# Ten high-half casts of weight pairs move from GpSimd to ScalarE, and the first pair of W_in is loaded and converted first

## The chip, the core and the metric

The kernel runs on one core of a Trainium2 chip. The core has TensorE (PE: matmuls; PEld: its weight loads), VectorE (DVE), ScalarE (ACT) and GpSimd (POOL), which run their own instruction streams in order and wait for each other by semaphores. SyncE (SP) issues all DMA transfers here. The metric is the time of one execution on the device in microseconds (us); "before" is the median of three runs.

## The reference

Attention with a decay and a causal mask, then two MLPs, over 4 x 576 tokens of 8 heads of 64:

```python
scores = np.where(causal, -1e9, scale * q @ k^T + cum[:, None] - cum[None, :])
x  = softmax(scores) @ v                 # (2304, 512)
h  = x @ w_in                            # w_in  (512, 2048)
g  = h * np.tanh(np.where(h > 20, h, np.log1p(np.exp(h))))
x2 = g @ w_out                           # w_out (2048, 512)
h2 = x2 @ w2_in                          # (512, 1024)
solu = h2 * softmax(h2)
out = layernorm(solu) * g_ln @ w2_out    # (1024, 512)
```

The weights come as float64, q, k, v and f as float32.

## The kernel before

Every matmul operand is kept as a pair of float16 halves, high and low (value = high + low), and each product is made of three matmuls: high x high, high x low, low x high.

**Weights.** W_in and W_out of the first MLP are cut into eight *pairs* each (two tiles of 128 x 512). A pair goes through three steps of class `Weight`. `load` brings the float64 values in with one DMA of 1,024 KB (L123); only two such buffers exist (`WB = 2`), shared by both weights, so a load waits until the conversion before the last has freed its buffer. `conv` makes float32 of the two 32-bit words of each float64 with three DVE instructions (L136, L138, L140) and then sums squares on PE (`gram`, L159). `split` scales the pair and makes its two halves by the function `split`, in one of three modes, chosen per pair by a digit of the strings `W1P` (W_in) and `W2P` (W_out):

- mode 0: ACT makes the scaled high half (L197), DVE the low half (L198);
- mode 1: ACT scales in place (L200), POOL casts the high half (L202), POOL subtracts to get the low half (L205);
- mode 2: as mode 1, but ACT casts the high half (L204).

The same function splits q, k and v. The scales of a group of four pairs (`bound`) come from `gram`.

**Order.** The code first issues loads of k, q, two pairs of W_in and v of the first batch, then the statistics of k (`stats`, `scales`), the splits of k and q, and starts attention. All other weight steps stand in a list `wsteps` that alternates two pairs of W_in and two of W_out; `wgo(n)` takes the next n steps, between attention steps. The first token block of the MLP (`up`: matmuls L754; `mish_a` to `mish_c`: L766 to L781; `down`: L798) is interleaved with these weight steps, since it needs them group by group. Later blocks of the MLP are interleaved with attention of the other batches, and the second MLP (lines about 1000) with the last ones. The program order is then rearranged by a scheduler in the build, which orders each engine's stream by its own model of time; the streams run on the chip exactly in that order.

Names: `win`, `wout` are the weights (the tile `wout` also lends its unused space to early k, q, v rows), `wi_r`, `wo_r` the float64 buffers, `kn`, `qn` the split k and q before their DMA transposes into `kt`, `qa`; `p`, `ph`, `pT` attention probabilities, their halves and their transposes; `h`, `ta`, `th`, `gt` the MLP's hidden values.

Of the kernel before, what the change touches and what calls it, by code (L numbers as in the profile page):

```python
# [40 lines left out]
WPF = 2  # L41
# [8 lines left out]
HI0 = "a"  # L50
HI1 = "pd"
SP1 = "0000001"
W1P = "00111111"
W2P = "10"
QKV = "002"
W0C = 1
S2Q = 3
S2R = 9
WB = 2
# [13 lines left out]
def rows_of(b, c):  # L73
    off = OFF[b]
    lo = max(128 * c, off)
    hi = min(128 * c + 128, off + S)
    return lo - 128 * c, hi - 128 * c, lo - off


def part_of(w, n):  # L80

    fr, c = divmod(2 * n, w.shape[0] // P)
    return w[c * P:(c + 2) * P, fr * 512:(fr + 1) * 512].rearrange("(s p) e -> p s e", p=P)


def later(tc, a, b):

    tc.add_manual_dep(
        getattr(a, "ins", a), getattr(b, "ins", b).name,
        mybir.DependencyInfo(mybir.DependencyClass.NoSync, mybir.DependencyReason.DATA),  # L90
        reason="issue order")
# [116 lines left out]
def emit(tc, q, k, v, f, w_in, w_out, w2_in, w2_out, g_ln, out):  # L208
# [81 lines left out]
    def load_raw(b, c, which, pool=None):  # L290
        r0, r1_, t0 = rows_of(b, c)
        n = r1_ - r0
        for nm in which:
            src = {"q": q, "k": k, "v": v}[nm]
            if pool is None:
                t = rawp.tile([P, DM], F32, tag="raw", name=f"raw{nm}_{b}_{c}")
            else:
                t = pool.pop()
            raw[nm, b, c] = t
            i = nc.sync.dma_start(  # L300
                t[r0:r1_].rearrange("p (h d) -> p h d", h=H),
                src[b, :, t0:t0 + n, :].rearrange("h s d -> s h d"),
            )
        return i

    def stats(b, c, which):

        if ("st", b) not in sc:
            sc["st", b] = att.tile([P, 2, NCH], F32, tag="st", name=f"st_{b}", bufs=2)
            nc.vector.memset(sc["st", b], 0.0)  # L310
        r0, r1_, _ = rows_of(b, c)
        for nm in which:
            jk = attd.tile([P, DM], F32, tag="x32", name=f"jk{nm}_{b}_{c}", bufs=1)
            nc.scalar.activation(
                jk[r0:r1_], raw[nm, b, c][r0:r1_], AF.Square,
                accum_out=sc["st", b][r0:r1_, "kv".index(nm), c:c + 1])
# [211 lines left out]
    def fin(b, i):  # L528
# [41 lines left out]
    W1 = Weight(  # L570
        tc, wst, "wi", win, NC1 * DFF // 512, lambda n: part_of(w_in, n), across, group=4,
        after=lambda: pend.get("pt"), gram=grams)
# [13 lines left out]
    def w1_split(n):  # L586
        g, r = divmod(n, W1.group)
        if r == 0:
            W1.bound(g)
            nc.vector.tensor_copy(wps[g], W1.p(g))  # L590
        W1.split(n, on_pool=int(W1P[n % len(W1P)]))

    def w2_split(n):
        g, r = divmod(n, W2.group)
        if r == 0:
            W2.bound(g)
            nc.vector.tensor_tensor(rho[:, g:g + 1], wps[g], W2.p(g), op=ALU.mult)
        W2.split(n, on_pool=int(W2P[n % len(W2P)]))

# [72 lines left out]
    wsteps, wdone = [], set()  # L672
    order = [(w, 2 * g + n) for g in range(4) for w in (W1, W2) for n in range(2)]
    for x in range(len(order) + WPF):
        if WPF <= x < len(order):
            wsteps.append((order[x][0].load, order[x][1]))
        if x >= WPF:
            w, n = order[x - WPF]
# [5 lines left out]
    def wgo(n):  # L684
        for _ in range(n):
            if wsteps:
                f, a = wsteps.pop(0)
                f(a)
                wdone.add((f, a))
# [7 lines left out]
    def pool0(c):  # L697
        return spare if c < 3 else None

    for c in range(NCH):  # L700
        load_raw(0, c, "k", pool0(c))
    for c in range(2):
        load_raw(0, c, "q", pool0(c))
    for n in range(WPF):
        W1.load(n)
    load_raw(0, 0, "v", pool0(0))
    for c in range(NCH):
        stats(0, c, "k")
    scales(0, "k")
# [6 lines left out]
    later(tc, load_raw(0, 2, "q", pool0(2)), first)  # L716
    wgo(W0C)
    for c in range(NCH):
# [156 lines left out]
    for hn in range(2 * (NF + 5)):  # L875
        n, half = divmod(hn, 2)
# [212 lines left out]
```

## Time and profile before

| | |
|---|---|
| median of three runs | 861.46 us (859.14 to 862.57) |
| profiled execution | 862.0 us, of which the span from first to last instruction is 860.2 us |
| busy, PE | 748.2 us (87% of the span) |
| busy, DVE | 606.7 us (71%) |
| busy, ACT | 549.1 us (64%) |
| busy, POOL | 442.2 us (51%) |
| mean granted clock of TensorE | 0.97 |

The shares are means over stages with different limits. The busy time of DVE and of POOL includes the time in which an instruction has started and is held up. About 1.8 us of the profiled time lie outside the span.

### The profile page before, as it was taken

What the parts mean: (1) busy time and instruction counts of PE and PEld (TensorE: products, weight loads), DVE (VectorE), ACT (ScalarE), POOL (GpSimd) and SP (SyncE); (2) the same over time, 40 slices, a digit from 0 to 9 for tenths busy, and PEclk for the clock granted to TensorE, in tenths of its full rate; (3) what the DMA queues carried; (4) which work ended last, traced back from release to release, by engine and by line L of the source; (5) the groups of instructions that cost most, each with busy time, mean ns of one, the idle gap of its engine ahead of it and who ended that gap; (6) DMA issues with size and microseconds to landing.
All of it is one profiled execution on the core that took longest, in us unless ns stands there. A gap on an engine that the chain in (4) does not pass through costs nothing.

```text
span 860.2 us, 16457 instructions
## 1 busy us (share of the span) xinstructions
PE 748.2 (87%) x6174; PEld 477.6 (56%) x6174; DVE 606.7 (71%) x1158; ACT 549.1 (64%) x1202; POOL 442.2 (51%) x341
## 2 busy tenths in 40 slices
PE   0555777789899988999999999986999999999997
PEld 0444545557567665676757677554555554444443
DVE  6699998597667878858887755599566444665451
ACT  5555657868778786888886767686955554333331
POOL 2268676755876576776678753228733122022110
PEclk9999997789999999999999999999999999999999
DMA  9999554487897889898896632841023423344543
GB/s 237 208 246 271 166 174 92 87 157 120 149 190 157 154 152 161 178 191 140 164 184 124 138 67 56 221 172 62 26 38 79 81 59 75 89 98 104 108 88 81
DMA packets 328571, 114.88 MB, mean 134 GB/s; under 512 B 317676, under 2 KB 317676, under 8 KB 328492
## 3 DMA queue, kind: packets, MB, share of 16 engines
q1 hardware_dynamic: 328492, 113.84, 63.2%
q8 instruction: 48, 0.79, 0.4%
q14 instruction: 31, 0.25, 0.1%
HBM read 46.59 MB, written 9.55 MB: 65 GB/s over the span
## 4 chain that ended last, share of the span: by engine, by line
PE 40%; DVE 23%; DMA 13%; ACT 9%; issue 8%; POOL 7%; SPq 1%; POOLq 0%; DVEq 0%; ACTq 0%
PE h L997 10%; PE o L1037 10%; PE x L798 9%; PE h L754 7%; DMA pT<-ph 4%; POOL ph L493 4%; DVE th L775 3%; DVE ta L771 2%; DMA w2i_r<-in_moe_w_in_dram 1%; DVE wout L140 1%; PE pv L524 1%; DVE ph L490 1%; DVE wout L138 1%; POOL gt L781 1%; DMA rawk<-in_k_dram 1%
## 5 line engine op out<-in xcount | busy, mean ns | idle before, releaser
L798 PE MATMUL x<-wout,gt 128*128 128x512 f16 x864 | 222.1, 392 | 21.8 <-ACT gt L780 10.1
L754 PE MATMUL h<-xT,win 128*128 128x256 f16 x1728 | 223.3, 279 | 2.3 <-POOL win L202 1.7
L493 POOL TENSOR_TENSOR ph<-p,ph 128x512 f16<-128x512 f32 (+4 forms) x120 | 159.6, 1334 | 80.3 <-ACT ph L492 32.8
L754 PEld LDWEIGHTS <-win 128*128 128x128 f16 x1728 | 170.3, 100 | 45.3 <-POOL win L202 1.8
L781 POOL TENSOR_TENSOR gt<-th,gt 128x512 f16<-128x512 f32 x72 | 91.9, 1277 | 100.5 <-ACT gt L780 100.5
L798 PEld LDWEIGHTS <-gt 128*128 128x128 f16 x864 | 81.6, 100 | 103.7 <-issue 14.9
L1025 POOL TENSOR_TENSOR z<-sl,z 128x1024 f16<-128x1024 f32 x18 | 38.7, 2150 | 138.1 <-DVE s2c L1004 111.3
L997 PE MATMUL h<-w,x2T 128*128 128x512 f16 x432 | 98.4, 380 | 2.9 <-POOL w L205 1.6
L1037 PE MATMUL o<-wo,zT 128*128 128x512 f16 x432 | 96.5, 379 | 0.5 <-DMA zT<-z 0.5
L410 PE MATMUL sp<-kt,qa 128*128 128x128 f16 (+3 forms) x480 | 71.8, 225 | 21.1 <-ACT p L454 11.9
L454 ACT ACTIVATE p<-sp,nm 64x64 f32<-64x64 f32 (+7 forms) x128 | 61.2, 484 | 41.0 <-DVE nm L452 23.3
L524 PE MATMUL pv<-vt,pT 128*128 128x64 f16 (+3 forms) x480 | 71.0, 203 | 15.4 <-DMA pT<-ph 10.7
L775 DVE SCALAR_TENSOR_TENSOR th<-ta,th 128x512 f32<-128x512 f32 x72 | 69.4, 965 | 21.1 <-ACT ta L774 20.9
L780 ACT CAST gt<-th 128x512 f16<-128x512 f32 x72 | 44.3, 615 | 48.6 <-DVE th L775 47.2
L411 PE MATMUL sp<-kt,qb 67*128 67x128 f16 (+3 forms) x480 | 72.9, 226 | 2.6 <-DVE qb L399 2.6
L997 PEld LDWEIGHTS <-x2T 128*128 128x128 f16 x432 | 42.3, 98 | 53.9 <-issue 4.0
L525 PE MATMUL pv<-vt,pT 128*128 128x64 f16 (+3 forms) x480 | 70.1, 198 | 1.0 <-DVE vt L198 1.0
L1037 PEld LDWEIGHTS <-zT 128*128 128x128 f16 x432 | 42.2, 98 | 51.5 <-DMA zT<-z 1.0
L526 PE MATMUL pv<-vt,pT 128*128 128x64 f16 (+3 forms) x480 | 70.3, 198 | 0.0
L772 ACT ACTIVATE ta<-ta 128x512 f32<-128x512 f32 x72 | 45.3, 631 | 36.0 <-DVE ta L771 35.8
L524 PEld LDWEIGHTS <-pT 128*128 128x128 f16 (+3 forms) x480 | 45.6, 102 | 36.7 <-DMA pT<-ph 20.5
L771 DVE TENSOR_SCALAR ta<-ta 128x512 f32<-128x512 f32 x72 | 53.7, 745 | 16.6 <-ACT ta L766 16.2
(235 smaller groups left out, 1455.8 us busy)
## 6 DMA issues: line engine op xcount, KB each, us to landing
wi_r<-in_moe_w_in_dram SPq DMA_DIRECT2D x8, 1024.0 KB
wo_r<-in_moe_w_out_dram SPq DMA_DIRECT2D x8, 1024.0 KB
rawk<-in_k_dram SPq DMA_DIRECT2D x25, 256.0 KB
rawv<-in_v_dram SPq DMA_DIRECT2D x25, 256.0 KB
x2d<-x2h SPq DMA_DIRECT2D x18, 256.0 KB
out_dram<-ro SPq DMA_DIRECT2D x18, 256.0 KB
w2i_r<-in_moe_w_in_dram SPq DMA_DIRECT2D x4, 1024.0 KB
w2o_r<-in_moe_w_out_dram SPq DMA_DIRECT2D x4, 1024.0 KB
```

Source lines behind the costliest of these rows:

```text
L410: nc.tensor.matmul(o, qa[:, h, r0:r1_], kc[:, h, a0:a1], start=True, stop=False)
L411: nc.tensor.matmul(o, qb_[:67, h, r0:r1_], kc[:67, H + h, a0:a1], start=False, stop=(c != i))
L493: nc.gpsimd.tensor_tensor(p4[:, :, 1], pv3, p4[:, :, 0], op=ALU.subtract)
L524: nc.tensor.matmul(o, pT[a0:a1, k, :m], vh, start=(c == 0), stop=False)
L526: nc.tensor.matmul(o, pT[a0:a1, k + 1, :m], vh, start=False, stop=(c == i))
L754: nc.tensor.matmul(ph, win[:, (fi // 4) * NC1 + c, col:col + P], x[:, lx * NC1 + c, :], start=(m == 0), stop=(m == 3 * NC1 - 1))
L771: nc.vector.tensor_scalar(ta, ta, E20, 1.0, op0=ALU.min, op1=ALU.add)
L775: nc.vector.scalar_tensor_tensor(th, ta, 2.5, th, op0=ALU.subtract, op1=ALU.mult)
L781: nc.gpsimd.tensor_tensor(gt[:, 1], th, gt[:, 0], op=ALU.subtract)
L798: nc.tensor.matmul(o, gt[:, lg, n % 2, t * P:(t + 1) * P], wout[:, fi, lw * 512:(lw + 1) * 512], start=(first and m == 0), stop=(last and ...
L997: nc.tensor.matmul(h[:, half * 512:(half + 1) * 512], x[:, lx * NC1 + c, :], self.w2[:, half * NC1 + c, lw * 512:(lw + 1) * 512], start=(n ...
L1037: nc.tensor.matmul(o, zT[:, lz * NF2 + c, :], self.wo[:, c, lw * 512:(lw + 1) * 512], start=(n == 0), stop=(n == 3 * NF2 - 1))
```

## The change

Two strings of digits and one count change, and the order of a few steps at the start:

```diff
-W1P = "00111111"
-W2P = "10"
+W1P = "00222222"
+W2P = "20"
-W0C = 1
+W0C = 2
@@ emit
+    W1.load(0)
     for c in range(NCH):
         load_raw(0, c, "k", pool0(c))
+    W1.load(1)
     for c in range(2):
         load_raw(0, c, "q", pool0(c))
-    for n in range(WPF):
-        W1.load(n)
     load_raw(0, 0, "v", pool0(0))
+    W1.conv(0)
+    wsteps.remove((W1.conv, 0))
     for c in range(NCH):
         stats(0, c, "k")
```

Six pairs of W_in (2 to 7) and four of W_out (0, 2, 4, 6) go from mode 1 to mode 2; by the instruction streams that makes ten casts. The first two pairs of W_in, and the other four of W_out, stay in mode 0. `W0C` is the number of weight steps taken before the statistics of v; with one conversion taken out of the list, two loads of W_out now stand there. The scheduler then rearranges all streams, PE's up to about 60% of its length.

SP at the very start issues the loads in this order before (`wi_r` is a pair of W_in, `wo_r` one of W_out, `dd` the decay terms, `kt` and `qa` transposes of k and q):

```order
L259 DMA ft<-in_f_dram 32x576
L300 DMA wout<-in_k_dram 128x8x64 x3
L300 DMA rawk_3_162<-in_k_dram 128x8x64
L300 DMA rawk_4_164<-in_k_dram 64x8x64
L300 DMA wout<-in_q_dram 128x8x64 x2
L123 DMA wi_r_168<-in_moe_w_in_dram 128x2x512
L123 DMA wi_r_170<-in_moe_w_in_dram 128x2x512
L300 DMA wout<-in_v_dram 128x8x64
L273 DMA dd<-d_118 32x1728
```

and in the change:

```order
L259 DMA ft<-in_f_dram 32x576
L123 DMA wi_r_159<-in_moe_w_in_dram 128x2x512
L300 DMA wout<-in_k_dram 128x8x64 x3
L300 DMA rawk_3_164<-in_k_dram 128x8x64
L300 DMA rawk_4_166<-in_k_dram 64x8x64
L123 DMA wi_r_168<-in_moe_w_in_dram 128x2x512
L300 DMA wout<-in_q_dram 128x8x64 x2
L300 DMA wout<-in_v_dram 128x8x64
L123 DMA wo_r_239<-in_moe_w_out_dram 128x2x512
L273 DMA dd<-d_118 32x1728
```

One pair now stands ahead of k, both stand ahead of q, and a pair of W_out already stands ahead of `dd`.

DVE at the start, from the decay terms (`d`) to the splits of k, in the change (before, the three rows of `wi_r_159` did not stand here, both conversions of W_in followed the first two splits of k (`kn`), and the first conversion of W_out came after them):

```order
L269 CAST d_118<-dt__116 32x576
L136 TENSOR_SCALAR win<-wi_r_159 128x1024
L270 TENSOR_TENSOR lf<-dt__116,d_118 32x576
L138 SCALAR_TENSOR_TENSOR win<-wi_r_159,win 128x1024
L271 CAST d_118<-lf 32x576
L140 SCALAR_TENSOR_TENSOR win<-wi_r_159,win 128x1024
L272 TENSOR_TENSOR d_118<-lf,d_118 32x576
L336 TENSOR_REDUCE sctk_196<-st_184 128x1
```

The first conversion moved ahead of the scale of k (`sctk`).

POOL in the weight stage, before (`ph` and `gt` are low halves of attention and MLP values):

```order
L493 TENSOR_TENSOR ph_2_6_949<-p_0_128,ph_2_6_949 128x3x128
L202 TENSOR_SCALAR win<-win 128x2x512
L205 TENSOR_TENSOR win<-win 128x2x512
L202 TENSOR_SCALAR win<-win 128x2x512
L205 TENSOR_TENSOR win<-win 128x2x512
L202 TENSOR_SCALAR wout<-wout 128x2x512
L205 TENSOR_TENSOR wout<-wout 128x2x512
```

The same weights in ACT's stream of the change, the last group of them (`L204` is the cast; `p` an exponential of attention, `ta` and `gt` steps of the MLP's hidden values, whose lines are two higher than before):

```order
L204 CAST win<-win 128x2x512
L200 ACTIVATE wout<-wout,wo_b 128x1024
L775 ACTIVATE ta_1659<-ta_1659,c_k_72 128x512
L454 ACTIVATE p_0_128,rsum_3_1062<-sp_148,nm_3_2_1150 128x512
L314 ACTIVATE jkv_4_1491,st_1037<-rawv_4_1428 128x512
L454 ACTIVATE p_1_129,rsum_3_1062<-sp_146,nm_3_3_1185 128x512
L204 CAST wout<-wout 128x2x512
L776 ACTIVATE ta_1659<-ta_1659 128x512
L204 CAST win<-win 128x2x512
L492 CAST ph_3_2_1158<-p_0_128 128x4x128
```

The POOL rows of L202 are gone, and each cast stands in ACT's queue between instructions of attention and of the MLP.

## Rows read from the trace of the kernel before

**Rows 1.** Stretches: length; PE, PEld, DVE, ACT, POOL busy; clock, DMA, GB/s.
```profile
0.00:20.00 20.00, 1.59 (x10) 1.27 (x10) 12.54 (x24) 11.54 (x22) 5.81 (x14) 1.00 1.07 248
20.00:44.00 24.00, 10.96 (x85) 9.34 (x86) 17.32 (x41) 14.37 (x44) 6.02 (x5) 1.00 1.02 207
44.00:60.00 16.00, 7.53 (x80) 6.09 (x80) 16.00 (x22) 8.28 (x19) 10.78 (x5) 1.00 1.00 255
60.00:141.00 81.00, 56.59 (x477) 40.71 (x475) 80.36 (x108) 46.03 (x84) 56.81 (x32) 0.94 0.64 176
141.00:156.00 15.00, 11.88 (x98) 7.92 (x99) 10.11 (x26) 12.24 (x26) 14.92 (x11) 0.73 0.64 132
156.00:220.00 64.00, 52.94 (x589) 39.61 (x588) 48.37 (x100) 49.56 (x127) 39.26 (x30) 0.85 0.76 134
220.00:500.00 280.00, 264.89 (x2859) 186.31 (x2860) 212.59 (x399) 218.63 (x536) 197.01 (x178) 0.98 0.85 157
```

**Rows 2.** Waits of DVE, 40 to 142 us: total, times, longest.
```profile
DVE vt L198 <- ACT vt L197: 2.1, 1, 2.1
```

**Rows 3.** Timeline of POOL: start us, us, instruction.
```profile
84.99 1.90 POOL L202 TENSOR_SCALAR win<-win 128x1024 f16<-128x1024 f32 x1
86.97 2.97 POOL L205 TENSOR_TENSOR win<-win 128x1024 f16<-128x1024 f32 x1
```

**Rows 4.** Timeline of DVE beside it.
```profile
82.97 3.02 DVE L138 SCALAR_TENSOR_TENSOR win<-wi_r,win 128x1024 int32<-128x1024 int32 x1
...
86.11 1.85 DVE L140 SCALAR_TENSOR_TENSOR win<-wi_r,win 128x1024 int32<-128x1024 int32 x1
```

**Rows 5.** Line 202 alone: POOL busy and count in two stretches.
```profile
60.00:141.00 81.00, 12.29 (x7) 0.94 0.64 176
141.00:156.00 15.00, 3.09 (x3) 0.73 0.64 132
```

**Rows 6.** Line 202: ns min/median/max, first and last start us.
```profile
L202 POOL TENSOR_SCALAR win<-win x6: 1039/1665/2006, 81.0 to 148.8; 128x1024 f16<-128x1024 f32 x6
```

**Rows 7.** One conversion, three DVE lines: the same columns.
```profile
L136 DVE TENSOR_SCALAR win<-wi_r x8: 674/776/1645, 14.5 to 119.5; 128x1024 int32<-128x1024 int32 x8
...
L138 DVE SCALAR_TENSOR_TENSOR win<-wi_r,win x8: 1205/1226/3018, 15.2 to 121.1; 128x1024 int32<-128x1024 int32 x8
...
L140 DVE SCALAR_TENSOR_TENSOR win<-wi_r,win x8: 1215/1226/3143, 17.3 to 122.8; 128x1024 int32<-128x1024 int32 x8
```

**Rows 8.** ACT groups, 128x1024 to f16: busy us, mean ns, idle before.
```profile
L149 ACT ACTIVATE w2i_r<-w 128x1024 f16<-128x1024 f32 x4 | 4.2, 1053 | 4.0 <-DVE w L140 4.0
...
L197 ACT ACTIVATE wout<-wout,wo_b 128x1024 f16<-128x1024 f32 x4 | 4.6, 1148 | 5.7 <-POOL wout L205 5.7
```

**Rows 9.** The chain that ended last, 142 to 158 us.
```profile
142.68 2.08 ACT win L200 x2
...
147.79 1.04 POOL wout L202
...
155.18 3.09 PE h L754 x14
```

**Rows 10.** Timeline of the start: start us, us, engine, instruction, idle before.
```profile
9.35 0.63 ACT L314 ACTIVATE jkk<-rawk 64x512 f32<-64x512 f32 x1 [0.21 <-DMA rawk<-in_k_dram]
...
11.82 0.72 ACT L200 ACTIVATE wout<-wout,scu 128x512 f32<-128x512 f32 x1 [1.75 <-DVE scu L346]
...
17.74 0.63 ACT L314 ACTIVATE jkv<-wout 128x512 f32<-128x512 f32 x1 [2.85 <-DMA wout<-in_v_dram]
```

**Rows 11.** Two stretches of 2 us at the start, columns of rows 1.
```profile
8.00:10.00 2.00, 0.00 (x0) 0.00 (x0) 0.55 (x1) 1.37 (x4) 0.00 (x0) 1.00 1.40 188
...
12.00:14.00 2.00, 0.00 (x0) 0.00 (x0) 0.82 (x2) 2.00 (x4) 0.00 (x0) 1.00 1.04 416
```

**Rows 12.** Waits of ACT, 44 to 160 us: total, times, longest.
```profile
ACT p L454 <- DVE nm L452: 13.8, 3, 5.8
ACT ta L772 <- DVE ta L771: 9.1, 2, 7.3
```

## The prediction

> **What bounds the kernel now.** I read the busy time by stretches first, because the shares over the whole span mix stages [rows 1]. Up to 44 us nothing is full. From 44 to 60 us DVE is busy 16.00 of 16 us and from 60 to 141 us 80.36 of 81, while PE is busy 7.5 of 16 and 56.6 of 81: for 97 us the kernel goes as fast as DVE, which converts the weights there. From 141 to 156 POOL is the full one (14.92 of 15). From 156 to 220 no engine is full (PE 52.9 of 64, ACT 49.6, DVE 48.4), and from 220 on PE is busy 264.9 of 280. So a microsecond taken from DVE's queue between 44 and 141 should bring everything behind it forward, as far as the stage from 156 to 220 lets it through. The waits of DVE say the same: its largest wait from 40 us on is 2.1 us, for ACT, once, before the full stage [rows 2].
>
> Next I looked at what DVE does while busy. One L138 alone takes 1.205 us, but up to 3.018 [rows 7]; L202 on POOL takes 1.039 alone and up to 2.006 [rows 6]. The timelines side by side show why. L138 of DVE runs 82.97 to 85.99, L202 of POOL 84.99 to 86.89, L140 of DVE 86.11 to 87.96, L205 of POOL 86.97 to 89.94 [rows 3, 4]. The ends alternate: 85.99 (DVE), 86.89 (POOL, 0.90 later), 87.96 (DVE, 1.07 later), 89.94 (POOL, 1.98 later). Each instruction advances only when the other engine's has ended, and the distances are about the times that they take alone. DVE and POOL here work as one queue. That makes L202, though it is on POOL, a cost of DVE.
>
> **The change part by part.** The sum is made against the profiled execution: 860.2 us span plus 1.8 around it, 862.0, which is 0.5 above the median.
>
> *Seven casts in the full stage.* Of the ten L202 that go, seven lie between 60 and 141 us, 12.29 us of POOL's busy time; three lie after, 3.09 us [rows 5]. Each of the seven took a turn of about 0.90 us out of the common queue (the distance above): 7 x 0.90 = 6.3 us. Lower bound nothing (if POOL's next instruction just fills the turn); upper bound 7 x 1.039 = 7.3. I take 6.3, since DVE is never without work there.
>
> The Trainium skill, "GPSIMD Engine Reference", section "Engine selection", says that elementwise work with one input runs on GpSimd at roughly line rate, which speaks against expecting anything of the move. The trace agrees on the speed (1.039 us alone on POOL). By that rule alone the seven casts would be worth nothing and the sum below would be 1.6 us; by the alternation they are worth 6.3 and it is 7.9, and I take the measurement.
>
> *What ACT pays.* A cast of 128x1024 from float32 to float16 on ACT is not in the trace; the nearest groups of that shape are L149 with 1.053 and L197 with 1.148 us [rows 8]. At 1.06 the seven casts are 7.4 us more on an engine that is busy 46.0 of 81 us there [rows 1], so it goes to about 53 of some 75: I cost it at nothing. The cover is ACT's idle time; if it were gone, the price would be up to 7.4.
>
> *Three casts after 141 us.* One is on the chain that ended last (L202, 1.04 us at 147.79), behind two L200 of ACT and ahead of the matmuls of `up` that wait for the weights until 155.18 [rows 9]. On POOL all three go (up to 3.1 saved), on ACT three come, and ACT is busy 12.24 of 15 there. Bounds 0 and 3.1; I take 1.0, the one that is on the chain.
>
> *The start.* One conversion alone is 0.674 + 1.205 + 1.215 = 3.1 us of DVE [rows 7]. Before, all eight of W_in and eight of W_out come after the scale of k. Now the first is done while DVE waits for k, so 3.1 us leave the later stage. Against that, the pair of 1,024 KB stands ahead of k. At 12 to 14 us, where the pairs are being loaded, the queues move 416 GB/s; at 8 to 10 us, with k and q, 188 [rows 11]. 1.05 MB at 416 GB/s is 2.5 us. The last statistics of k start at 9.35 us when their data land, and the first q is scaled at 11.82, when DVE has the scale [rows 10]; both go 2.5 us later, to about 11.9 and 14.3. q itself goes behind both pairs. Before, k, q, both pairs and then v land in that order, v at 17.74 [rows 10]; v's 0.26 MB at 188 GB/s take 1.4 us, so now q lands at about 16.3, 2.0 behind the new time of the scale. In that time DVE has the second conversion of W_in and the first splits of k to do, whose data are there. So the whole start slides by about 2.5 us, with one conversion more behind it: a gain of 3.1 - 2.5 = 0.6. Bounds: 3.1 gained, if the idle time of DVE (6.7 of 24 us between 20 and 44 [rows 1]) swallows the slide, and a loss of 1.4, if q's whole delay (16.3 - 11.8 = 4.5) comes through.
>
> A pair of W_out is now issued ahead of `dd` and of the transposes of k; it waits for the first conversion, which is done before the scale of k, so SP is not held; its transfer of 2.5 us runs while DVE converts. I cost it at nothing; uncovered it would be 2.5, inside the bounds above.
>
> *What is late next.* From 156 to 220 us PE idles 11 of 64 us [rows 1] on chains of ACT, DVE and transposes that are about as long as before. They start earlier and end earlier. The reordered streams behind them hold the same instructions, and I cost that at nothing; the price of a worse order is a rival.
>
> **Sum:** 6.3 + 1.0 + 0.6 = 7.9 us. 862.0 - 7.9 = 854.1, less the 0.5 to the median: **853.6 us**, 0.9% faster.
>
> **The rivals.**
>
> *A. The gain stops at the next stage.* For: 156 to 220 us has no full engine, so it is set by latency, and ACT, which gets three more casts just ahead of it, is busy 77% there; the streams are reordered. Or the casts weigh nothing, since POOL's next instruction takes their turn. The rule of the Trainium skill named above ("GPSIMD Engine Reference", "Engine selection") would say that. Against: the alternation of ends, and that the chains from 156 on begin with the end of the weights. Then only the start's 0.6 is left: 861.46 - 0.6 = 860.9, no change.
>
> *B. Slower: the casts are caught in ACT's queue.* On POOL a cast waited only for its own scaling. On ACT it stands behind instructions that wait for DVE: between 44 and 160 us ACT waits for DVE in L454 three times, 13.8 us together, and in L772 twice, 9.1 together [rows 12], 4.6 each on average. In the new stream a cast of the last group stands behind two L454. If one such wait of 4.6 is put in front of each of the three groups of W_in that change, and `up` waits for it, 13.8 us are lost: 862.0 - 7.9 + 13.8 - 0.5 = 867.4. It decides from 7.9 / 3 = 2.6 us per group on. Against: while `up` waits, DVE still has conversions to do, and they set the end of the stage.
>
> *C. More than forecast.* All bounds on the good side: 7.3 + 3.1 + 3.1 = 13.5 us, 848 us. TensorE's granted clock is 0.73 of full speed from 141 to 156 us (time at both its levels, 1.2 and 2.4 GHz) against 0.94 before [rows 1]; at 0.94 its 11.88 busy us there would be 9.2, 2.7 less: 845.3 at the very best.
>
> **How the numbers follow.** The three runs lie within 0.4%, so 0.5% (4.3 us) is about what can be told from no change: faster means under 857.2, slower above 865.8. The forecast and C together have 0.60 (C alone 0.10), A 0.25, B 0.15. Faster 0.60, same 0.25, slower 0.15. The range that leaves out no more than two in ten reaches from 846 (C) over A to 865, short of B. The likeliest case's own range is 849 to 858.
>
> **What would show it.** Right: no L202 on `win` or `wout`, ten L204 of about 1.06 us on ACT; DVE full from about 44 us to about 134 instead of 141, with L138 and L140 shorter on average; the `up` matmuls after the last weights at about 147 instead of 155; from there on the same busy shares, shifted. The last statistics of k start near 11.9 us, the scaling of q near 16.3. Wrong: ACT waiting for DVE directly ahead of an L204 while POOL idles at L205 (B); DVE ending its full stage early and PE idling more than 11 us afterwards (A); DVE's full stage as long as before with POOL's busy time down by 15 us (A, casts without weight); a start of the full stage more than 3 us later than 44 (the start mis-sized).

## The result, and the profile of the changed kernel

| | before | changed |
|---|---|---|
| median | 861.48 us (859.14 to 863.27, 5 runs) | 869.8 us (867.8 to 873.6, 5 runs) |
| ratio, 95% interval | | 1.010 (1.0078 to 1.0122) |
| span of the profiled execution | 860.2 us | 871.6 us (the execution of 873.6, the slowest of the five) |

The change makes the kernel 1.0% slower; the forecast was 0.9% faster.

The stretches of the changed kernel, in the columns of [rows 1]:

```profile
0.00:20.00 20.00, 1.60 (x10) 1.28 (x10) 13.72 (x25) 10.78 (x20) 6.21 (x14) 1.00 1.05 260
20.00:44.00 24.00, 12.20 (x94) 10.25 (x95) 18.95 (x39) 13.54 (x43) 5.67 (x5) 1.00 1.20 214
44.00:60.00 16.00, 6.82 (x79) 5.86 (x80) 15.70 (x32) 10.90 (x21) 9.74 (x3) 1.00 0.63 180
60.00:141.00 81.00, 52.72 (x454) 38.42 (x454) 69.01 (x103) 51.48 (x95) 48.10 (x27) 0.92 0.77 199
141.00:156.00 15.00, 10.94 (x93) 7.99 (x92) 8.87 (x19) 13.04 (x23) 9.99 (x6) 0.75 0.32 62
156.00:220.00 64.00, 53.40 (x543) 37.87 (x542) 39.12 (x90) 47.86 (x122) 33.12 (x27) 0.81 0.60 114
220.00:500.00 280.00, 260.31 (x2810) 184.78 (x2809) 221.84 (x400) 212.44 (x524) 199.28 (x176) 0.98 0.88 159
```

DVE's work in the full stage did shrink: 69.01 us between 60 and 141, 11.4 less than before, though 103 instructions stand there now and 108 before. But DVE is no longer full there, and PE, which should have profited, did less: 52.72 against 56.59. From 220 to 500 us PE is busy 4.6 us less than before.

The operations themselves came as forecast. Groups of line 204 (busy us, mean ns):

```profile
L204 ACT CAST win<-win 128x1024 f16<-128x1024 f32 x6 | 6.3, 1046 | 0.0
L204 ACT CAST wout<-wout 128x1024 f16<-128x1024 f32 x4 | 4.2, 1039 | 0.0
```

The second and third step of the W_in conversions (ns min/median/max, first and last start):

```profile
L138 DVE SCALAR_TENSOR_TENSOR win<-wi_r,win x8: 1205/1210/1224, 7.7 to 118.7; 128x1024 int32<-128x1024 int32 x8
...
L140 DVE SCALAR_TENSOR_TENSOR win<-wi_r,win x8: 1206/1210/3146, 9.2 to 121.2; 128x1024 int32<-128x1024 int32 x8
```

Ten casts of 1.04 us on ACT (1.06 forecast), and without POOL's casts the W_in rows of L138 take at most 1.224 us instead of 3.018 [rows 7]; those of L140 still take up to 3.146. The timeline of the start:

```profile
12.10 0.63 ACT L314 ACTIVATE jkk<-rawk 64x512 f32<-64x512 f32 x1
...
15.95 0.71 ACT L200 ACTIVATE wout<-wout,scu 128x512 f32<-128x512 f32 x1
```

The last statistics of k start at 12.10 (11.9 forecast), the first q is scaled at 15.95 (16.3 forecast) [rows 10]. So the lengths of the operations and the slide of the start came about as forecast, and the total was wrong by 16 us. The early end of the weight stage did not come: the `up` matmuls behind the last weights were to start at about 147 instead of 155.18 [rows 9], and they start at 156.19 (a row of PE's timeline):

```profile
156.19 3.22 PE L756 MATMUL h<-xT,win 128*128 128x256 f16 x28
```

To see where, I follow TensorE's work in time: for each matmul line, the count up to a moment times what one takes when they stand close (L754 0.108 us, L798 0.216, scores 0.081, pv 0.056; 24 of L754 take 2.78 us), summed and set against the same sum of before. Each column is one execution, in us ahead (+) or behind (-); the other columns are experiments below.

| up to us | changed | e1 | p1 | p2 | r1 | s2 | t1 | t2 |
|---|---|---|---|---|---|---|---|---|
| 100 | -5.0 | +0.7 | +0.9 | -0.4 | +0.6 | +1.6 | -0.6 | +0.1 |
| 160 | -2.5 | +3.6 | +2.5 | +2.2 | +2.2 | +5.2 | +2.4 | +3.9 |
| 260 | -4.8 | +10.2 | +5.6 | +7.0 | +6.6 | +10.8 | +8.0 | +8.9 |
| 340 | -2.6 | +11.1 | +4.8 | +9.1 | +4.6 | +6.9 | +5.1 | +6.9 |
| 420 | -10.5 | +2.3 | +5.0 | +2.1 | -4.9 | +7.7 | +5.4 | +6.2 |
| 500 | -10.8 | +1.8 | +3.9 | +0.8 | -4.9 | +7.8 | +2.4 | +5.8 |
| 700 | -11.9 | +1.2 | +3.4 | +0.3 | -7.5 | +8.1 | +2.6 | +6.3 |

The changed kernel loses 5 us early, makes half of it good, and loses 8 between 340 and 420 us, in instructions that the change doesn't touch. Its profiled execution is 3.8 us slower than its median, so its column shows somewhat more than its usual loss.

### The profile page after: what moved, and what is told of

It is laid out like the page before. It is cut to its first block, busy times and chain, and to the rows that moved or that the text cites. A ratio compares the mean times of both kernels' runs of the same rounds, so it can differ in the third digit from the quotient of the medians.

```text
span 871.6 us, 16444 instructions
## 1 busy us (share of the span) xinstructions
PE 751.4 (86%) x6174; PEld 480.5 (55%) x6174; DVE 603.6 (69%) x1158; ACT 556.1 (64%) x1212; POOL 430.7 (49%) x331
## 4 chain that ended last, share of the span: by engine, by line
PE 38%; DVE 20%; DMA 11%; ACT 10%; issue 9%; POOL 7%; SPq 1%; DVEq 0%; POOLq 0%; ACTq 0%
PE h L999 10%; PE o L1039 10%; PE x L800 8%; PE h L756 6%; DMA pT<-ph 4%; POOL ph L493 3%; DVE th L777 3%; DVE ta L773 2%; DVE ph L490 2%; DMA w2i_r<-in_moe_w_in_dram 2%; ACT p L454 1%; POOL gt L783 1%; DVE nm L452 1%; DMA qa<-qn 1%; ACT ta L776 1%
## 5 line engine op out<-in xcount | busy, mean ns | idle before, releaser
L756 PEld LDWEIGHTS <-win 128*128 128x128 f16 x1728 | 172.9, 101 | 53.7 <-issue 8.6
L777 DVE SCALAR_TENSOR_TENSOR th<-ta,th 128x512 f32<-128x512 f32 x72 | 72.9, 1013 | 31.7 <-ACT ta L776 29.7
L524 PE MATMUL pv<-vt,pT 128*128 128x64 f16 (+3 forms) x480 | 71.5, 204 | 22.2 <-DMA pT<-ph 21.2
L524 PEld LDWEIGHTS <-pT 128*128 128x128 f16 (+3 forms) x480 | 46.0, 102 | 45.0 <-DMA pT<-ph 29.7
```

What stands on the lines that cost most here:

```text
L524: nc.tensor.matmul(o, pT[a0:a1, k, :m], vh, start=(c == 0), stop=False)
L756: nc.tensor.matmul(ph, win[:, (fi // 4) * NC1 + c, col:col + P], x[:, lx * NC1 + c, :], start=(m == 0), stop=(m == 3 * NC1 - 1))
L777: nc.vector.scalar_tensor_tensor(th, ta, 2.5, th, op0=ALU.subtract, op1=ALU.mult)
```

## The experiments

Theory after the result: the reordered streams cost what the moved work gains. Rivals: the casts are caught in ACT's queue, or the start costs more than forecast.

**Parts alone.** *e1* takes only the two strings of digits (casts on ACT). *e2* takes the start and `W0C = 2` with the casts on POOL, *e8* the start with `W0C = 1`, *e3* the whole change with `W0C = 1`.

> Only the ten casts move to ACT; the start is that of before. Theory 1 (the early conversion lets the first pair of W_out get ahead of attention in ACT's queue, ACT waits for POOL's low half, and DVE runs dry): no such place here, so the casts show what they are worth alone, 853 to 861 us, no wait of ACT for POOL's L205 above 5 us. Theory 2 (the casts themselves, caught in ACT's queue, stall POOL and then the weights): 866 to 871 us, with POOL waiting over 5 us for L204.

> Only the start moves: first pair of W_in ahead of k, converted at once, and two weight steps ahead of the statistics of v; the casts stay on POOL. Theory 1: as slow as the change or worse, 868 to 873 us, with ACT's wait for POOL's L205 of W_out of about 8 us near 55 to 63 us and heads 5 to 7 of row block 2 about 30 us later than before. Theory 2: 858 to 862 us.

> The change with one weight step instead of two ahead of the statistics of v. In ACT's stream the first pair of W_out is then scaled behind the fourth head of row block 2 again, and heads 5 and 6 are ahead of the MLP. Theory 1: the loss is gone, 852 to 861 us. Theory 2: it stays, 866 to 871 us.

> The start of the change with one weight step, casts on POOL as before. Theory 1: 858 to 863 us (the start alone, without the overtaking, is worth about nothing, since the 2.5 us of the early load eat the 3.1 us of the early conversion). Theory 2: the same. If it is at 868 or more, the early load or the early conversion is itself the loss, and both theories are wrong.

Measured, against 860.15 us of before on the same chip: e1 859.57 (0.999, 0.9977 to 1.0004), e2 868.99 (1.0106, 1.0086 to 1.0126), e3 866.48 (1.0091, 1.0059 to 1.0123), e8 872.61 (1.0144, 1.0114 to 1.0175). The casts alone, in the order that the scheduler gives them, cost nothing and gain nothing; everything with the new start is slower. That a pair of W_out overtakes attention in ACT's queue because of `W0C = 2` (theory 1) is not the cause: ACT's wait for POOL's L205 of W_out, 6.5 us in e2, is 0.4 in e8, and e8 is the slowest. Theory 2 falls by e1. The table adds that e1 was 11 us ahead at 340 us and lost 9 of them by 420.

**Order held.** To separate work from order, the kernel traces itself twice: once as another version, whose order is read off, and once as itself, with edges of issue order (no waits) that hold every engine to the order read:

```diff
+    order = traced(inputs, ORDER_OF)[1]
+    nc, _, arrays = traced(inputs, RUN, order)
...
+            for e, keys in order.items():
...
+                for a, b in zip(keys, keys[1:]):
+                    tc.add_manual_dep(
+                        at[b], at[a].name,
+                        mybir.DependencyInfo(mybir.DependencyClass.NoSync, mybir.DependencyReason.DATA),
+                        reason="issue order")
```

Instructions that the change moves (casts, first loads, first conversion) stay free. *p1* is e1 in the order of before, *p2* the work of before in the order of e1, *p4* the new start, *p3* the whole change in the order of before. In p3 and p4 the slot that the first conversion left in `wsteps` stays empty, so that `W0C = 1`:

```diff
+    if EARLY:
+        W1.conv(0)
+        wsteps[wsteps.index((W1.conv, 0))] = (int, 0)
```

> The ten casts on ACT, and every other instruction of every engine held in the order in which the kernel before has it (edges of issue order alone, no waits). Theory O (the casts gain what the stage 44 to 141 us showed, and the order that the scheduler makes of the changed program loses it again between 360 and 500 us): about 852 us, -7 to -10, with TensorE's work at 500 us still 7 to 10 us ahead of before. Rival W (the gain is taken back by the work itself: engines that were hidden become the limit after 360 us, whatever the order): 859 to 861, as the casts alone gave (859.6).

> The work of the kernel before, casts on GpSimd, in the order that the scheduler gave the program with the casts on ACT. Theory O: the order alone costs what the casts gained, so 865 to 870 us. Rival W: order costs nothing, 859 to 862.

> The whole change (ten casts on ACT, first pair of W_in loaded ahead of k, second ahead of q, first one converted at once), every other instruction in the order of the kernel before; the slot that the first conversion left in the weight steps stays empty, so the later steps stand beside the same attention steps as before. Theory O: 851 to 855 us, as the prediction had it (853.6), since the start moves only about 3 us of conversion and slides the first scores by 2.5. Rival S (the early load and conversion themselves cost, through the later start): 861 to 870, and above the casts alone in the same order by what the start costs.

> The start of the change alone (early load, early conversion), casts on GpSimd, every other instruction in the order of the kernel before. Theory O: 860 to 863 us, no more than the 2.5 us by which the first scores come later. Rival S (the start itself costs 8 to 11, as it did with the scheduler's own order): 868 to 873.

Measured: p1 858.65 (0.9981, 0.9965 to 0.9997), p2 861.71 (1.002, 1.0001 to 1.0039), p3 860.62 (1.0007, 0.9987 to 1.0026), p4 862.34 (1.002, 1.0 to 1.004), before 860.23. The start itself costs 0.2%, 1.7 us, the whole change nothing. So order is most of the loss. But theory O fell for the casts: in the order of before they bring 1.6 us, not 8, and p3 lies between its two ranges. It fell for p2 too: e1's order costs the old work about 1.5 us, not 5 to 10. So in that one order the casts are worth 1.002 - 0.999, 0.3% or 2.6 us (p2 against e1), little more than the noise. The full stage of p1 (columns of [rows 1]):

```profile
60.00:141.00 81.00, 58.51 (x479) 42.11 (x478) 73.15 (x119) 55.51 (x96) 42.09 (x26) 0.90 0.67 180
```

The third step of its W_out conversions (ns min/median/max, first and last start):

```profile
L140 DVE SCALAR_TENSOR_TENSOR wout<-wo_r,wout x8: 1211/1514/2426, 29.9 to 136.1; 128x1024 int32<-128x1024 int32 x8
```

DVE's largest wait from 60 to 141 us (total, times, longest):

```profile
DVE wi_b L176 <- PE sp L327: 4.0, 1, 4.0
```

The stretches up to the end of that last conversion, from the start and from 44 us, before and then in p1 (columns of [rows 1]):

```profile
0.00:139.78 139.78, 75.97 (x642) 56.94 (x642) 125.00 (x192) 79.60 (x166) 78.20 (x54) 0.96 0.81 202
...
44.00:139.78 95.78, 63.42 (x547) 46.34 (x546) 95.14 (x129) 53.69 (x102) 66.37 (x35) 0.95 0.70 192
```

```profile
0.00:137.29 137.29, 76.24 (x642) 57.87 (x642) 117.64 (x192) 86.53 (x173) 60.50 (x47) 0.95 0.82 206
...
44.00:137.29 93.29, 62.98 (x536) 46.69 (x536) 86.04 (x127) 59.28 (x106) 48.41 (x28) 0.93 0.72 194
```

And a stretch of 2 us and rows of PE's timeline, all of p1:

```profile
94.00:96.00 2.00, 2.00 (x12) 1.40 (x10) 0.00 (x0) 0.80 (x2) 2.00 (x2) 0.50 0.91 373
```

```profile
92.33 5.00 PE L754 MATMUL h<-xT,win 128*128 128x256 f16 x23
97.17 0.28 PE L327 MATMUL sp<-wi_b,ones 128*128 128x1 f32 x2
...
115.08 1.89 PE L754 MATMUL h<-xT,win 128*128 128x256 f16 x8 [3.10 <-ACT win L204]
...
150.42 2.41 PE L754 MATMUL h<-xT,win 128*128 128x256 f16 x16 [2.74 <-ACT win L204]
...
153.65 3.94 PE L754 MATMUL h<-xT,win 128*128 128x256 f16 x28
```

DVE's 80.36 us became 73.15, 7.2 less for seven casts, where 6.3 were forecast. The fixed window holds 119 instructions now and 108 before; DVE's instructions up to the last conversion, the same ones in the same order in both, take 125.0 us before and 117.6 in p1, 7.4 less. But the last conversion starts at 136.1, only 2.5 us sooner than in the kernel before (138.6), and the `up` matmuls behind the last weights start at 153.65, 1.5 sooner than 155.18: DVE now idles 7.3 us of that stretch instead of 0.6, 4.0 in one piece for a sum on PE that the bound of a weight group needs. That sum (L327) stands in PE's stream behind 23 `up` matmuls, which take 5.0 us, with the granted clock at 0.50 from 94 to 96 us. And PE twice waits for a cast that stands on ACT behind other work, 5.8 us together, the mechanism of rival B.

**Is it ACT's queue; which part of the order.** *p5* is p1 with each cast put directly behind the L200 that it reads (POOL's 19.8 us of waiting for L204, that its expectation names, are six waits in p1's trace, not nine). *q0* is p3's program with no order held, *r1* holds only the instructions written ahead of the MLP's second block, *r2* only those from there on:

```diff
+            up1 = [i for i, n in enumerate(names) if n[1] == UP][12 * NF1]
+            part = set(names[:up1] if PART == "early" else names[up1:])
```

> The ten casts on ACT in the order of the kernel before, as in the run with the casts alone in that order (858.65), but each cast stands directly behind the scaling on ACT that it reads (L200), not some instructions later. Theory Q (the casts' gain was caught in ACT's queue: there TensorE waited 3.10 us at 115 and 2.74 us at 150 for casts that stood behind other work on ACT, and GpSimd 19.8 us in nine waits): both waits of TensorE go, 853 to 856 us. Rival L (the chain from conversion over the bound to the scale is what the stage goes by, and a cast that comes earlier only lengthens ACT's queue for the exponentials): 858 to 861.

> The same traced program as the whole change in the order of before (860.62), with no order held: the scheduler sets every engine's. Theory O (order is what makes the change slow): 866 to 870 us, as the change with its own two forms of this place gave (869.8 and 866.5). Rival G (the empty slot and one load step fewer, by which the held one differs from the change, were what helped): 860 to 862.

> As the run before, with the order of the kernel before held only among instructions written ahead of the MLP's second block (about the first 165 us), the later ones free. If the loss lies in the early order (attention of row block 1 and 2 pushed back, 4 to 5 us of TensorE's work by 100 us): 860 to 863. If in the later one (another 5 us between 340 and 420 us): 865 to 868.

> The other half: order held only among instructions written from the MLP's second block on, the earlier ones free. If the loss lies in the early order: 865 to 868. If in the later one: 860 to 863. Both halves near 864 to 865 would say that each has its part.

Measured, against 860.99: p5 861.13 (0.9999, 0.9981 to 1.0018), q0 867.72 (1.0092, 1.0059 to 1.0124), r1 869.75 (1.0111, 1.0079 to 1.0143), r2 863.32 (1.0023, 1.0004 to 1.0042). Theory Q fell: PE's two waits are gone in p5 and nothing is gained. The same program costs 0.9% with a free order and nothing in the order of before, and of the two halves it is the late order that makes the loss against before; r1 is even 2 us beyond its range, 865 to 868.

What a bad place in it looks like, from r1. First stretches of 2 us (columns of [rows 1]), then rows of the timelines of PE and of DVE, then two groups of matmuls on PE from 405.5 to 415.6 (busy us, mean ns; line numbers are eight higher than before: L806 is `down`, L762 `up`, L828 and L835 the eviction of a finished block):

```profile
310.00:312.00 2.00, 0.00 (x0) 0.00 (x0) 1.11 (x4) 2.00 (x10) 0.00 (x0) 0.92 1.17 84
312.00:314.00 2.00, 1.70 (x26) 1.44 (x27) 0.93 (x2) 1.97 (x7) 1.10 (x1) 0.50 1.08 236
...
318.00:320.00 2.00, 2.00 (x28) 1.64 (x27) 2.00 (x3) 0.76 (x3) 1.64 (x2) 0.87 0.54 122
...
412.00:414.00 2.00, 0.00 (x0) 0.10 (x1) 2.00 (x5) 1.55 (x3) 0.85 (x1) 1.00 1.20 260
414.00:416.00 2.00, 0.37 (x1) 0.10 (x1) 2.00 (x5) 2.00 (x9) 0.30 (x1) 0.52 0.70 133
416.00:418.00 2.00, 2.00 (x6) 0.60 (x4) 1.97 (x4) 2.00 (x11) 0.89 (x2) 0.50 0.40 135
418.00:420.00 2.00, 2.00 (x28) 1.56 (x27) 2.00 (x1) 2.00 (x6) 2.00 (x2) 0.50 0.04 11
```

```profile
312.30 0.23 PE L524 MATMUL pv<-vt,pT 64*128 64x64 f16 x1 [2.66 <-DMA pT<-ph]
...
403.55 1.89 PE L806 MATMUL x<-wout,gt 128*128 128x512 f16 x8
...
415.63 2.72 PE L806 MATMUL x<-wout,gt 128*128 128x512 f16 x6 [3.74 <-DVE x2h L835]
...
407.39 0.68 DVE L828 TENSOR_REDUCE x2m<-x 128x1 f32<-128x512 f32 x1
...
414.84 0.73 DVE L835 SCALAR_TENSOR_TENSOR x2h<-x,x2m,x2h 128x512 f16<-128x512 f32 x1
```

```profile
L762 PE MATMUL h<-xT,win 128*128 128x256 f16 x32 | 4.0, 273 | 0.0
L524 PE MATMUL pv<-vt,pT 128*128 128x64 f16 (+1 forms) x10 | 1.3, 196 | 0.5 <-DMA pT<-ph 0.5
```

At the end of its fourth block the MLP frees the one PSUM tile of a half (128 of a block's 256 tokens; pool `psx`, one buffer) only when DVE has done L835, 8.2 us after the eviction began with L828, since DVE's queue holds other work between the two. In that time PE has 32 `up` matmuls and an attention part of ten L524 to do, and then stands still 3.74 us for L835. In p3, the same program in the order of before, more stands between the two `down` groups, 407.3 to 418.3 us:

```profile
L762 PE MATMUL h<-xT,win 128*128 128x256 f16 x50 | 5.8, 273 | 0.0
L524 PE MATMUL pv<-vt,pT 128*128 128x64 f16 (+1 forms) x20 | 2.6, 196 | 0.5 <-DMA pT<-ph 0.5
```

There PE goes from one to the other without a wait of that kind, although L835 ends no sooner after its L828. The other runs agree: from 340 to 425 us PE's waits for this eviction (`x2h`), 4.4 us in r1, are 4.1 in q0, 3.9 in e3, 2.2 in e2, 2.0 in e1 and p2 and 1.5 in e8, and at most 0.5 in before and in all runs that hold the late order of before; of those with a free late order only the changed kernel has none. Two of these rows (total, times, longest; q0, then s4):

```profile
PE x L806 <- DVE x2h L835: 4.1, 1, 4.1
```

```profile
PE x L806 <- DVE x2h L835: 0.2, 1, 0.2
```

With each of r1's two stops TensorE's granted clock goes to 0.50, its lower level of 1.2 GHz: from 312 to 318 us half of 5.7 busy us, 2.9, is lost besides the stop of 2.66, and from 416 to 420 half of 4.0, 2.0, besides the 3.74 (estimates, from the busy times and clocks shown).

**Holding the late order alone.** If that is it, the casts can keep the 10 us that e1 had at 340 us. *s1*, *s2* and *s3* are e1 with the order of before held from the MLP's third, fourth and fifth block on (`CUT`, in the place of `NF1` = 16 above, is 32, 48, 64), *s4* is q0 held from the fourth on.

> Casts on ACT; order of the kernel before held among instructions written from the MLP's third block on (about 260 us), free ahead of it. Theory H (the loss at 410 us is a matter of order, and what TensorE is ahead by then stays): the free early order has TensorE 4 to 10 us ahead by 260 us, so 852 to 857. Rival E (being ahead early only makes the engines wait for each other later, since VectorE is full at 400 to 420 us): 858 to 861.

> As the run before, held from the MLP's fourth block on (about 330 us). Theory H: TensorE is 9 to 11 us ahead by 340 us in the free order, so 850 to 856. Rival E: 858 to 861.

> As the run before, held from the MLP's fifth block on (about 390 us), the place of the loss itself included. Theory H: 850 to 856 if the stall near 410 us stands behind the cut, 858 to 861 if ahead of it. Rival E: 858 to 861.

> The whole change, order of the kernel before held from the MLP's fourth block on, free ahead of it. If the loss lies at the fourth block's end near 410 us: 861 to 864. If it lies ahead of it (near 310 us, or spread over blocks two and three): 865 to 869.

Measured, against 859.69: s1 853.78 (0.9934, 0.9916 to 0.9951), s2 853.47 (0.9929, 0.9906 to 0.9952), s3 854.52 (0.9945, 0.9924 to 0.9965), s4 859.54 (0.9996, 0.9982 to 1.0011). Theory H holds and rival E falls: s1 to s3 beat both kernels. The stretch from 400 to 420 us, e1 first and then s2:

```profile
400.00:420.00 20.00, 15.65 (x174) 11.21 (x171) 19.84 (x32) 15.73 (x49) 13.51 (x13) 0.92 0.82 172
```

```profile
400.00:420.00 20.00, 19.34 (x263) 15.44 (x262) 17.61 (x41) 18.26 (x55) 16.05 (x14) 1.00 0.86 169
```

PE is busy 3.7 us more in s2. Holding from the fifth block on is already enough, and the whole change loses nothing against before when held from the fourth.

**Casts or early order?** *t1* is the work of before and *t2* the whole change, both in s2's order (the casts and, in t2, what the start moves stay free again).

> Casts on GpSimd as in the kernel before, every instruction in the order of the run with 853.5 us. Theory R (the early order is worth most of it, the casts what they gave in the order of before, 1.6 us): 854 to 857. Rival K (the casts themselves carry the gain, which only an order that keeps it shows): 858 to 861.

> The whole change, every instruction that it doesn't move in the order of the run with 853.5 us. If the start costs what it did in the order of before (2.0 to 2.1 us): 855 to 856. If it costs what the run with the free early order has above the casts alone (6 us): 859 to 860.

Measured, against 860.25: t1 858.87 (0.9979, 0.9961 to 0.9996), t2 855.24 (0.9934, 0.9919 to 0.995). In this order the casts are worth 0.9979 - 0.9929, 0.5% or 4.3 us (the two half-widths together make this uncertain by about 2.5 us), and the order alone 1.8. That is nearer rival K. The new start costs 0.9934 - 0.9929, less than can be told. t2 differs from s4 only in the early order: s4 has the scheduler's own for the whole change, t2 that of e1. That is worth 0.9996 - 0.9934, 5.3 us. So of the 13.6 us between the same program in q0 (1.0092) and in t2, 8.3 lie in the late order and 5.3 in the early one.

## Why the prediction was wrong

- **The step that failed** is "The reordered streams behind them hold the same instructions, and I cost that at nothing; the price of a worse order is a rival." No rival had a price for it. One program (p3 against q0) costs 0.0085 more, 7.3 us, in the scheduler's order than in that of before, and 13.6 us more than in that of t2; the change as it was given (1.010) lies with q0 (1.0092). By s4 against q0 the loss of 0.0096 goes when the instructions from the MLP's fourth block on are held. In the changed kernel itself the largest stop of PE between 340 and 420 us is one for a transpose, and the clock falls with it; a row of PE's timeline, and a stretch behind it:

```profile
388.95 0.20 PE L524 MATMUL pv<-vt,pT 64*128 64x64 f16 x1 [2.42 <-DMA pT<-ph]
```

```profile
392.00:394.00 2.00, 2.00 (x11) 1.41 (x10) 0.73 (x1) 2.00 (x8) 1.59 (x2) 0.50 0.76 171
```

  Which instruction's place makes that transpose late was not tried; the changed kernel has no wait for the eviction there, so r1's stops show the kind, not this one.
- **Seven casts, 6.3 us.** As a size on DVE about right (7.4 for the same instructions in p1, the upper bound 7.3), as a gain in time only in part. "I take 6.3, since DVE is never without work there" was the mistake: with the casts gone DVE ran out of work and waited 4.0 us for PE. The end of the conversions moved 2.5 us, and the kernel 1.6 in the order of before, 2.6 in e1's, 4.3 in s2's. The rule that I set against the trace, that of the Trainium skill, "GPSIMD Engine Reference", section "Engine selection", would have given nothing: the gains in the order of before and in e1's are too near the noise to speak against that, the 4.3 us in s2's do.
- **What ACT pays, nothing.** Not contradicted: PE's waits for casts (rival B) are real in p1, but without them (p5) the time is no better. What the casts cost the rest of ACT's queue was not measured by itself.
- **Three casts after 141 us, 1.0.** Not seen. The last low half of W_in on POOL starts at 153.00 before and at 151.03 in p1, 2.0 us sooner, and the conversions ahead of it already end 2.5 sooner (rows of POOL's timeline, before, then p1):

```profile
153.00 2.12 POOL L205 TENSOR_TENSOR win<-win 128x1024 f16<-128x1024 f32 x1
```

```profile
151.03 2.13 POOL L205 TENSOR_TENSOR win<-win 128x1024 f16<-128x1024 f32 x1
```

- **The start, a gain of 0.6.** The slide was right to 0.4 us. The conversion taken ahead did not pay for it: the start alone costs 1.7 us in the order of before, a little beyond the bound of 1.4 (by the interval of p4, 0 to 3.4).
- **Rivals.** For the casts alone A was near, a gain that is lost on the way, though not where A put it: DVE waits inside its own stage, and PE idles 10.6 us from 156 to 220 in the changed kernel, not over 11. The time of B (867.4) lies near the measured one, but for another reason.

So the sum of 7.9 us was too large, and what the work brings depends on the order: 3.9 us in s2's (t2 against t1, 0.9934 and 0.9979; uncertain by about 2), nothing that can be told in that of before (p3). The 5.7 us of t2 against before hold 1.8 that the order brings without the change (t1).

## What to carry to other kernels

Where a scheduler in the build orders the streams, a change of a few instructions is two changes, and the second can be the larger one. Time it once with the old order held before judging the first: that tells work from order, and a partly held order may be the better kernel. Where PE is nearly full, look for what stands between a `down` group that ends a block and the next one that needs its tile: r1's stop of 3.74 us there cost about 5.7, by the estimate above, since the clock fell too.

## What the hardware showed that I had not expected

The prediction had DVE and POOL take turns. Its own example already has an exception that it passed over, a short instruction of DVE that starts and ends inside POOL's L202 of 84.99 to 86.89 [rows 3]:

```profile
85.91 0.28 DVE L174 TENSOR_REDUCE wo_b<-gram 128x1 f32<-128x128 f32 x1
```

The changed kernel has a larger counter-example, on POOL:

```profile
53.23 7.54 POOL L543 TENSOR_TENSOR xh<-x,xh 128x512 f16<-128x512 f32 x1 [3.29 <-DVE xh L542]
...
80.38 1.15 POOL L543 TENSOR_TENSOR xh<-x,xh 128x512 f16<-128x512 f32 x1
```

An instruction of 1.15 us took 7.54. From 53.08 to 59.77 us DVE ran ten instructions one behind the other, all near the shortest length of their kind, and POOL's ended 1.0 us after the last. So POOL doesn't always get its turn between two of DVE, and an engine that waits for POOL then waits for a whole train of DVE's: the W_out pair behind it in POOL's queue (L205) ended at 62.85, ACT stood 7.99 us for that, and PE 8.33 for an exponential behind it in ACT's queue:

```profile
65.83 0.27 PE L410 MATMUL sp<-kt,qa 128*128 128x128 f16 x1 [8.33 <-ACT p L454]
```

This is what theory 1 named, and it fits the early loss: in e2, the other run with `W0C = 2`, ACT waits 6.5 us there, and by the count of the table TensorE is 5.6 us behind at 100 us, as the changed kernel is, while e3 and e8 are about 1 ahead.

The Trainium skill, "SBUF — State Buffer", section "SBUF: two separate sides", says that GpSimd and certain instructions of VectorE (those in a mode of two ports, or with two SBUF inputs while GpSimd reads SBUF) share a pair of ports as an exclusive lock, which the one that starts first gets for the whole instruction. The waiting agrees. That who starts first goes first does not, if the profile's starts are the ones meant: L543 began at 53.23, before nine of the ten. Which of the ten took the ports, and when, the trace does not show.
